# Linear attention block: uneven halves of the state, three head groups folded inside the second half, and another order of the first loads

## The chip, the cores and the metric

The kernel runs on one core of a Trainium2 chip. The metric is the device time in microseconds (us) of one execution. Each execution also leaves a span, from its first to its last recorded instruction, and a granted TensorE clock (1.0 is full speed). The chip has a slower state: a run is called slow when it is over 1.5% above the fastest run of the same kernel.

Engine names in the profile: PE is TensorE (matmuls), PEld its weight loads, DVE is VectorE, ACT is ScalarE, POOL is GpSimd, SP is SyncE, which here only issues DMAs. A *bank* is one of the eight numbered places (0 to 7, 512 columns each) that the kernel writes matmul results to. It is in use until another engine has read the result.

## The reference

```python
B, S, D = 1, 2048, 640;  H = 32;  Dh = 20          # all inputs bf16
q, k, v = split(x @ wqkv)                          # 32 heads of 20
phi = lambda t: where(t > 0, t + 1, exp(t)) + 1e-6
pq, pk = phi(q), phi(k)
kv  = einsum("bhsd,bhse->bhde", pk, v);  z = sum over s of pk
num = pq @ kv;  den = pq . z + 1e-6
out = (num / den) @ wo
```

The kernel uses associativity. It never forms V. It makes the state P = x^T pk (640 x 640), then kv = Wv^T P for each group of heads, masks it to the heads' own 20 x 20 blocks, multiplies it with Wo ("folding Wo", giving w2), and the output is pq (divided by den) times w2.

## The kernel before: the parts that matter

The operations are added in program order to one queue per engine, and semaphores follow from what each reads and writes. **An engine runs its own queue strictly in the order in which the operations were added.** An operation that is not ready holds up everything behind it (seen below: VectorE stood idle for 2.00 us with ready operations queued behind one that was not).

```python
def p_step(h, st, ds=range(5)):          # PE: 5 matmuls for x tile st, P half h (320 columns)
    for d in ds: matmul(bank(d, HALF), xn[tile st, chunk d], pk[st, half h],
                        start=(st == 0), stop=(st == 15))
def p_out(h):                            # P half h -> pt: banks 0,2,4 by ACT, banks 1,3 by DVE
def q_tile(sbk, c, b):                   # PE: 5 matmuls of 512 columns into bank b
    ACT: eq = exp(bank b)
    DVE: eq = min(eq, 1) + 1e-6
    DVE: pq[sbk, c] = max(bank b, 0) + eq          # only now is bank b free
def z_steps():                           # DVE: 7 additions over pk (1280 wide), then zs; ACT zh; DVE zl
def z_finish(b):                         # PE: z per feature; DVE: zc, then five zb = hm * zc
def inverse(pair):                       # PE: den; ACT: ln, exp; SP: spread rd;
                                         #   queues 10 normalisations pq *= rd (DVE)
# ... cut ...
for st in range(2, 16):                  # half one: P holds banks 0-4 open
    p_step(0, st)
    if st % 3 == 2: next z step
    if st in (3, 7, 10, 13): next_q(0)   # Q tiles use banks 5, 6, 7 in turn
p_out(0); next_q(0); next_q(0)
for st in range(16):                     # half two
    p_step(1, st)
    if st in (0, 1, 3): next z step
    if st in (0, 2, 4, 6, 11): next_q(0)
    if st == 7: z_finish(take())
    if st == 9: inverse(0)
    if st == 14: work(4)                 # 4 normalisations
p_out(1); next_q(2); next_q(2)           # Q tile, each followed by 2 normalisations
kv_group(0); kv_mask(0)                  # all six groups of 120 columns
# ... then folding of groups 0 to 5 with the last Q tiles in between, then 16 output tiles
```

## Time and profile before

| | before |
|---|---|
| time, median of 4 runs | 104.77 us (104.47 to 107.26) |
| span of the profiled run, clock | 103.7 us, 1.0 |
| first P matmul to first output matmul | 28.2 to 79.1: 50.9 us |

Lines to recognise in this kernel: L268 is K, L295 is P, L321 to L334 is a Q tile (matmuls, exp, VectorE's two steps), L340 the z additions, L310 the evacuation of P by VectorE, L384 zb, L396 Wv times P, L413 its mask, L420 the folding, L446 den, L478 the output.

The first view is the chain that ended last, in order of time. Its columns are the start, the length, and what ran.

```profile
5.92 2.35 PE ps L268 x16
...
28.38 2.72 PE ps L295 x20
...
34.90 1.08 PE ps L321 x5
...
79.16 2.78 PE ps L478 x20
```

Twenty P matmuls of 320 columns take 2.72 us, so one issues every 0.136 us, and a Q tile of five 512-column matmuls takes 1.08 us (0.216 each). With these spacings everything TensorE has to do between first P and first output matmul adds up to 47.6 us: 21.8 (P) + 21.6 (Q) + 1.6 (Wv times P) + 1.6 (folding) + 0.7 (den) + 0.3 (z). I call this stretch **the middle**. It took 50.9 us. The Trainium skill ("Perfetto Trace Analysis", Identifying the Most-Contended Engine) warns that matmul busy time is no good measure, because pipelined instructions look smaller in the trace than they are. Here the warning holds, but the records look larger: one 320-column record lasts 0.299 us, over twice its spacing.

The second view is TensorE's waits (the warm-up's line at its top left out). Columns: engine and line, what it waited for, us in total, number of waits, longest.

```profile
PE ps L420 <- DVE kvt L413: 0.8, 1, 0.8
PE ps L446 <- DVE zb L384: 0.6, 1, 0.6
PE ps L420 <- DVE w2g L426: 0.5, 1, 0.5
PE ps L295 <- DVE pt L310: 0.4, 1, 0.4
...
PE ps L321 <- issue: 0.2, 1, 0.2
```

Five short waits lie in the middle, 2.5 us together.

### The profile page before, as it was taken

How to read it: one execution, taken by the hardware profiler on the slowest of the kernel's cores; microseconds unless marked ns; L12 is line 12 of the kernel's file. 1: busy time of each engine (PE TensorE's matmuls, PEld its weight loads, DVE VectorE, ACT ScalarE, POOL GpSimd, SP SyncE). 2: the span in 40 equal slices, each digit the busy share in tenths (PEclk: the TensorE clock that was granted, in tenths of full speed). 3: DMA queues.
4: the chain of work that ended last, by engine and by line, in shares of the span. 5: the costliest groups of instructions: out<-in, count | busy, mean ns of one | idle time of the engine just before them, and what ended most of it. 6: DMA issues, size and time to landing. Idle time of an engine off the chain costs nothing.

```text
span 103.7 us, 1779 instructions
## 1 busy us (share of the span) xinstructions
PE 97.6 (94%) x700; PEld 65.0 (63%) x705; DVE 70.6 (68%) x142; ACT 37.8 (36%) x68; POOL 2.5 (2%) x13
## 2 busy tenths in 40 slices
PE   6989999999999999989999799969799999999992
PEld 2467777777776666646666466736355677777771
DVE  0226988888895587799978409797979625866331
ACT  4005555444422112462224131625646253332222
POOL 6300000000000000000000000000000000000000
PEclk9999999999999999999999999999999999999999
DMA  2999998999960000000000013000550135533333
GB/s 67 290 304 189 216 267 255 376 364 363 234 123 0 3 0 0 0 0 3 6 0 0 0 33 68 0 6 0 157 156 3 63 89 141 193 126 126 126 126 126
DMA packets 17076, 11.93 MB, mean 115 GB/s; under 512 B 8621, under 2 KB 17069, under 8 KB 17069
## 3 DMA queue, kind: packets, MB, share of 16 engines
q1 hardware_dynamic: 16349, 11.22, 39.2%
q10 hardware_dynamic: 720, 0.61, 1.9%
q8 instruction: 5, 0.08, 0.3%
q14 instruction: 2, 0.02, 0.1%
HBM read 5.90 MB, written 2.62 MB: 82 GB/s over the span
## 4 chain that ended last, share of the span: by engine, by line
PE 68%; DVE 18%; DMA 4%; ACT 4%; issue 3%; ACTq 0%; DVEq 0%
PE ps L478 21%; PE ps L268 21%; PE ps L295 13%; PE ps L321 10%; DVE pq L334 5%; DVE za L340 4%; DMA wk<-in_wqkv_dram 4%; DVE eq L331 2%; ACT eq L329 2%; DVE pq L471 1%; PE ps L446 1%; DVE zs L361 1%; PE ps L420 1%; ACT pt L307 1%; DVE zl L366 1%
## 5 line engine op out<-in xcount | busy, mean ns | idle before, releaser
L295 PE MATMUL ps<-pk,xn 128*128 128x320 bf16 x160 | 23.9, 299 | 0.4 <-DVE pt L310 0.4
L321 PE MATMUL ps<-xT,wqn 128*128 128x512 bf16 x95 | 23.0, 379 | 0.4 <-issue 0.2
L268 PE MATMUL ps<-wk,xT 128*128 128x320 bf16 x160 | 22.7, 301 | 0.5 <-DMA wk<-in_wqkv_dram 0.3
L478 PE MATMUL ps<-w2p,pq 128*128 128x320 bf16 (+1 forms) x165 | 22.1, 295 | 0.0
L329 ACT ACTIVATE eq<-ps 128x512 bf16<-128x512 f32 x20 | 11.9, 597 | 23.9 <-PE ps L321 23.4
L295 PEld LDWEIGHTS ps<-pk,xn 128*128 128x128 bf16 x160 | 15.4, 98 | 8.2 <-DVE pt L310 0.9
L268 PEld LDWEIGHTS ps<-wk,xT 128*128 128x128 bf16 x160 | 15.4, 98 | 7.2 <-DMA wk<-in_wqkv_dram 1.2
L478 PEld LDWEIGHTS ps<-w2p,pq 128*128 128x128 bf16 x165 | 15.8, 98 | 6.4 <-DVE pq L334 0.4
L281 ACT ACTIVATE ek<-ps 128x640 bf16<-128x640 f32 x16 | 11.3, 704 | 15.8 <-PE ps L268 15.0
L321 PEld LDWEIGHTS ps<-xT,wqn 128*128 128x128 bf16 x100 | 11.6, 118 | 7.8 <-issue 0.3
L503 DVE CAST osb<-ps 128x320 bf16<-128x320 f32 (+1 forms) x16 | 7.7, 481 | 10.1 <-PE ps L478 10.1
L334 DVE SCALAR_TENSOR_TENSOR pq<-ps,eq 128x512 bf16<-128x512 f32 x20 | 13.8, 692 | 0.7
L286 DVE SCALAR_TENSOR_TENSOR pk<-ps,ek 128x640 bf16<-128x640 f32 x16 | 13.2, 825 | 0.6
L331 DVE TENSOR_SCALAR eq<-eq 128x512 bf16<-128x512 bf16 x20 | 5.8, 289 | 9.8 <-ACT eq L329 9.8
L500 ACT CAST osb<-ps 128x320 bf16<-128x320 f32 (+1 forms) x17 | 7.0, 416 | 13.2 <-PE ps L478 11.7
L471 DVE TENSOR_TENSOR pq<-pq,rd 128x512 bf16<-128x512 bf16 x20 | 7.7, 417 | 0.0
L195 DVE COPY xT<-ps 128x256 bf16<-128x256 bf16 (+1 forms) x8 | 2.2, 320 | 6.5 <-PE ps L190 6.5
L283 DVE TENSOR_SCALAR ek<-ek 128x640 bf16<-128x640 bf16 x16 | 5.2, 325 | 2.0 <-ACT ek L281 2.0
L340 DVE TENSOR_TENSOR za<-pk 128x1280 f32<-128x1280 bf16 x4 | 5.9, 1481 | 0.0
L340 DVE TENSOR_TENSOR za<-za 128x1280 f32<-128x1280 f32 x3 | 4.4, 1481 | 0.0
L258 PE MATMUL ps<-const-bfloat16-1.0 128*128 128x512 bf16 (+1 forms) x8 | 3.1, 546 | 0.8 <-PEq L652 0.8
L420 PE MATMUL ps<-wog,kvt 120*120 120x320 bf16 (+1 forms) x12 | 2.4, 308 | 1.3 <-DVE kvt L413 0.8
(37 smaller groups left out, 32.6 us busy)
## 6 DMA issues: line engine op xcount, KB each, us to landing
out_dram<-osb SPq DMA_DIRECT2D x15, 160.0 KB, 1.8
xn<-in_x_dram SPq DMA_DIRECT2D x3, 640.0 KB, 8.0
wqn<-in_wqkv_dram SPq DMA_DIRECT2D x1, 800.0 KB, 5.6
wv<-in_wqkv_dram SPq DMA_DIRECT2D x1, 800.0 KB, 11.2
wog<-in_wo_dram SPq DMA_DIRECT2D x1, 750.0 KB, 13.2
w2p<-w2g SPq DMA_DIRECT2D x5, 150.0 KB
rd<-rdc SPq DMA_DIRECT2D x8, 64.0 KB, 2.2
wk<-in_wqkv_dram SPq DMA_DIRECT2D x3, 160.0 KB, 3.9
```

The source lines that it names most:

```text
L268: r = e.matmul(bank(b + h, HALF), xT[:, c * S + 128 * st:c * S + 128 * st + 128], wk[:, c * D + HALF * h:c * D + HALF * (h + 1)], start=(c ...
L281: P.add("act", lambda e: e.activation(fold(t[:, :]), two_banks(b), ACTF.Exp), reads=banks + ["table"], writes=[("ek", st % 3)])
L286: P.add("dve", lambda e: e.scalar_tensor_tensor(fold(pk[:, st * D:(st + 1) * D]), two_banks(b), 0.0, fold(t[:, :]), ALU.max, ALU.add), rea ...
L295: r = e.matmul(bank(d, HALF), xn[:, st * D + 128 * d:st * D + 128 * d + 128], pk[:, st * D + HALF * h:st * D + HALF * (h + 1)], start=(st ...
L321: r = e.matmul(bank(b), wqn[:, d * D:(d + 1) * D].rearrange("p (q c) -> p c q", c=NC_)[:, c, :], xT[:, d * S + BK * sbk:d * S + BK * (sbk ...
L329: P.add("act", lambda e: e.activation(t[:, :], bank(b), ACTF.Exp), reads=[("bank", b), "table"], writes=[("eq", i)])
L331: P.add("dve", lambda e: e.tensor_scalar(t[:, :], t[:, :], 1.0, 1e-6, ALU.min, ALU.add), reads=[("eq", i)], writes=[("eq", i)])
L334: P.add("dve", lambda e: e.scalar_tensor_tensor(pq[:, c * S + BK * sbk:c * S + BK * (sbk + 1)], bank(b), 0.0, t[:, :], ALU.max, ALU.add), ...
L340: P.add("dve", lambda e: e.tensor_tensor(d_ap, a, b, ALU.add), reads=ra + rb, writes=[dst])
L471: P.add("dve", lambda e: e.tensor_tensor(v, v, rd[i][:, BK * h:BK * (h + 1)], ALU.mult), reads=[("rd", i, 2 * h), ("rd", i, 2 * h + 1), (" ...
L478: r = e.matmul(bank(b, hi - lo), pq[:, c * S + 128 * st:c * S + 128 * st + 128], w2p[:, c * D + lo:c * D + hi], start=(c == 0), stop=(c == ...
L503: P.add("dve", lambda e: e.tensor_copy(osb[j][:, lo:hi], bank(b, hi - lo)), reads=[("bank", b)], writes=keys)
```

## The change

The intent was to hide three of the six head groups' work (Wv times P and folding) inside half two of P. Half one becomes 360 columns, which is exactly three groups of 120, so these groups' state is complete before half two begins. For this the z steps and den moved later, eight Q tiles instead of five went into half two, zb went to GpSimd, and all copies of w2 went to ScalarE. Apart from that, the start loads x tile 0 whole and Wk block 0 beside it.

```diff
+    PW, PO = (3 * GW, D - 3 * GW), (0, 3 * GW)            # 360 and 280 columns
-            for eng, lo in (("sp", 0), ("act", HALF)):    # x tile 0 in two halves
-                ...
-            for eng, what in (("sp", "w01 w23 w34 x24"), ("act", "x12 w12 w45")):
+            for eng, what in (("sp", "x01 w12 w23 w45 x24"), ("act", "w01 x12 w34")):
-                P.add("dve", lambda e, c=c: e.tensor_scalar(
+                P.add("pool", lambda e, c=c: e.tensor_scalar(   # zb
-        order = "k00 t1 k01 k02 k10 k11 k12 k03 k04 k13 t2 k14 t3"
+        order = "k00 k01 t1 k02 k03 k10 k11 k12 k04 k13 t2 k14 t3"
         for st in range(2, NT):
             p_step(0, st)
-            if st % 3 == 2:
+            if st in (3, 6, 9, 12):
                 zst.pop(0)()
-            if st in (3, 7, 10, 13):
+            if st in (4, 7, 10, 13):
                 next_q(0)
         ...
         for st in range(NT):
             p_step(1, st)
-            if st in (0, 1, 3):
+            if st == 2:
+                b = take()
+                kv_group(0, b)                  # groups 0-2
+                kv_mask(0, b)
+            if st in (1, 4, 7, 10):
                 zst.pop(0)()
-            if st in (0, 2, 4, 6, 11):
+            if st % 2:
                 next_q(0)
-            if st == 7:
+            if st in (6, 8, 10):
+                g = st // 2 - 3
+                w2_split(g, take)               # fold group g, two small banks
+                w2_rows(g)
+            if st == 12:
                 z_finish(take())
-            if st == 9:
+            if st == 14:
                 inverse(0)
-            if st == 14:
-                work(4)
         p_out(1)
-        ... (two Q tiles with 2 normalisations each, then all six groups)
+        small[:] = [5, 6, 7]
+        next_q(0)
+        kv_group(1, 4)                          # groups 3-5
+        kv_mask(1, 4)
+        next_q(0)
+        for g in range(3, NG):
+            w2_group(g, 2 * (g - 3))
+            w2_rows(g)
+        small[:] = [6, 7, 0, 1]
         while qs:
-            next_q(1)
+            next_q(2)
```

More of the change, by code (lines that the diff above doesn't have):

```diff
@@ L225, in load_wk @@
             P.add("act", lambda e: e.add_instruction(tl), writes=["table"])
-            for eng, lo in (("sp", 0), ("act", HALF)):
-                P.add(eng, lambda e, lo=lo: e.dma_start(
-                    xn[:, lo:lo + HALF], x[0, 0:128, lo:lo + HALF]),
-                    writes=[("xn", 0, lo)], dma=True)
-            for eng, what in (("sp", "w01 w23 w34 x24"), ("act", "x12 w12 w45")):
+            for eng, what in (("sp", "x01 w12 w23 w45 x24"), ("act", "w01 x12 w34")):
                 for k in what.split():
@@ L241, in xn_keys @@
         def xn_keys(t):
-            return [("xn", t)] if t else [("xn", 0, 0), ("xn", 0, HALF)]
+            return [("xn", t)]
         def load_rest():
@@ L295, in mm @@
                     r = e.matmul(
-                        bank(d, HALF), xn[:, st * D + 128 * d:st * D + 128 * d + 128],
-                        pk[:, st * D + HALF * h:st * D + HALF * (h + 1)],
+                        bank(d, PW[h]), xn[:, st * D + 128 * d:st * D + 128 * d + 128],
+                        pk[:, st * D + PO[h]:st * D + PO[h] + PW[h]],
                         start=(st == 0), stop=(st == NT - 1))
@@ L304, in p_out @@
             for d in range(NC_):
-                dst = pt[:, d * D + HALF * h:d * D + HALF * (h + 1)]
+                dst = pt[:, d * D + PO[h]:d * D + PO[h] + PW[h]]
                 if d % 2 == 0:
-                    P.add("act", lambda e, d=d, dst=dst: e.copy(dst, bank(d, HALF)),
+                    P.add("act", lambda e, d=d, dst=dst: e.copy(dst, bank(d, PW[h])),
                           reads=[("bank", d)], writes=[("pt", d, h)])
                 else:
-                    P.add("dve", lambda e, d=d, dst=dst: e.tensor_copy(dst, bank(d, HALF)),
+                    P.add("dve", lambda e, d=d, dst=dst: e.tensor_copy(dst, bank(d, PW[h])),
                           reads=[("bank", d)], writes=[("pt", d, h)])
@@ L383, in z_finish, with kv_group, mm, kv_mask @@
             for c in range(NC_):
-                P.add("dve", lambda e, c=c: e.tensor_scalar(
+                P.add("pool", lambda e, c=c: e.tensor_scalar(
                     zb[:, 32 * c:32 * c + 32], hm[:, :], zc[:, c:c + 1], None, ALU.mult),
                     reads=["hm", "zc"], writes=[("zb", c)])
-        def kv_group(b):
-            for lo, hi, bb in ((0, 4, b), (4, 6, b + 1)):
-                def mm(e, lo=lo, hi=hi, bb=bb):
-                    for g in range(lo, hi):
-                        n = gsz[g]
-                        m = 128 if g < 5 else n
-                        for d in range(NC_):
-                            r = e.matmul(
-                                bank(bb, n, off=128 * (g - lo), parts=m),
-                                wv[:, d * D + GW * g:d * D + GW * g + m],
-                                pt[:, d * D + GW * g:d * D + GW * g + n],
-                                start=(d == 0), stop=(d == NC_ - 1))
-                    return r
-                P.add("pe", mm, reads=["wv", "wvpad"] + [("pt", d, h) for d in range(NC_)
-                                                         for h in range(2)],
-                      writes=[("bank", bb)])
-        def kv_mask(b):
-            for lo, n, bb, w in ((0, 4, b, GW), (4, 1, b + 1, GW), (5, 1, b + 1, 40)):
-                src = ps[0:w, BK * bb + 128 * (lo % 4):BK * bb + 128 * (lo % 4) + 128 * n] \
+        def kv_group(h, b):
+            def mm(e):
+                for g in range(3 * h, 3 * h + 3):
+                    n = gsz[g]
+                    m = 128 if g < 5 else n
+                    for d in range(NC_):
+                        r = e.matmul(
+                            bank(b, n, off=128 * (g % 3), parts=m),
+                            wv[:, d * D + GW * g:d * D + GW * g + m],
+                            pt[:, d * D + GW * g:d * D + GW * g + n],
+                            start=(d == 0), stop=(d == NC_ - 1))
+                return r
+            P.add("pe", mm, reads=["wv", "wvpad"] + [("pt", d, h) for d in range(NC_)],
+                  writes=[("bank", b)])
+        def kv_mask(h, b):
+            for lo, n, w in ((0, 3, GW),) if h == 0 else ((3, 2, GW), (5, 1, 40)):
+                src = ps[0:w, BK * b + 128 * (lo % 3):BK * b + 128 * (lo % 3 + n)] \
                     .rearrange("p (g j) -> p g j", j=128)[:, :, 0:w]
@@ L413, in kv_mask, with w2_half @@
                 P.add("dve", lambda e, src=src, m=m, dst=dst: e.tensor_tensor(
-                    dst, src, m, ALU.mult), reads=[("bank", bb), "bm"],
+                    dst, src, m, ALU.mult), reads=[("bank", b), "bm"],
                     writes=[("kvt", g) for g in range(lo, lo + n)])
+        def w2_half(g, h, b):
+            n = gsz[g]
+            P.add("pe", lambda e: e.matmul(
+                bank(b, HALF, parts=n), kvt[0:n, GW * g:GW * g + n],
+                wog[0:n, g * D + HALF * h:g * D + HALF * (h + 1)], start=True, stop=True),
+                reads=[("kvt", g), "wog", "wog5"], writes=[("bank", b)])
         def w2_group(g, b):
@@ L419, in w2_group, with w2_split @@
             for h in range(2):
-                P.add("pe", lambda e, h=h: e.matmul(
-                    bank(b + h, HALF, parts=n), kvt[0:n, GW * g:GW * g + n],
-                    wog[0:n, g * D + HALF * h:g * D + HALF * (h + 1)], start=True, stop=True),
-                    reads=[("kvt", g), "wog", "wog5"], writes=[("bank", b + h)])
-            dst = fold(w2g[0:n, g * D:(g + 1) * D])
-            if g % 2:
-                P.add("dve", lambda e: e.tensor_copy(dst, two_banks(b, parts=n)),
-                      reads=[("bank", b), ("bank", b + 1)], writes=[("w2g", g)])
-            else:
-                P.add("act", lambda e: e.copy(dst, two_banks(b, parts=n)),
-                      reads=[("bank", b), ("bank", b + 1)], writes=[("w2g", g)])
+                w2_half(g, h, b + h)
+            P.add("act", lambda e: e.copy(
+                fold(w2g[0:n, g * D:(g + 1) * D]), two_banks(b, parts=n)),
+                reads=[("bank", b), ("bank", b + 1)], writes=[("w2g", g, 0), ("w2g", g, 1)])
+        def w2_split(g, take):
+            n = gsz[g]
+            for h in range(2):
+                b = take()
+                w2_half(g, h, b)
+                lo = g * D + HALF * h
+                P.add("act", lambda e, b=b, lo=lo: e.copy(
+                    w2g[0:n, lo:lo + HALF], bank(b, HALF, parts=n)),
+                    reads=[("bank", b)], writes=[("w2g", g, h)])
         def w2_rows(g):
@@ L437, in w2_rows @@
                 w2g[0:gsz[g], g * D:(g + 1) * D]),
-                reads=[("w2g", g)], writes=[("w2p", g)], dma=True)
+                reads=[("w2g", g, 0), ("w2g", g, 1)], writes=[("w2p", g)], dma=True)
         def den(pair, b):
@@ L586, in bass_standalone__linear_attn_block__prompt_kernel, with pair @@
             p_step(1, st)
-            if st in (0, 1, 3):
+            if st == 2:
+                b = take()
+                kv_group(0, b)
+                kv_mask(0, b)
+            if st in (1, 4, 7, 10):
                 zst.pop(0)()
-            if st in (0, 2, 4, 6, 11):
+            if st % 2:
                 next_q(0)
-            if st == 7:
+            if st in (6, 8, 10):
[3 more added lines that the diff above has]
+            if st == 12:
                 z_finish(take())
-            if st == 9:
+            if st == 14:
                 inverse(0)
-            if st == 14:
-                work(4)
         assert not zst
         p_out(1)
-        next_q(2)
-        next_q(2)
-        kv_group(0)
-        kv_mask(0)
-        small[:] = [5, 6, 7, 4]
-        def fold_wo(g):
-            w2_group(g, 2 * ((g + 1) % 2))
-            w2_rows(g)
-        next_q(0)
-        fold_wo(0)
-        fold_wo(1)
-        next_q(0)
-        fold_wo(2)
-        fold_wo(3)
-        next_q(0)
-        fold_wo(4)
-        fold_wo(5)
-        while qs:
-            next_q(1)
-        out_tile(0, 0)
+        small[:] = [5, 6, 7]
[5 more added lines that the diff above has]
+            w2_group(g, 2 * (g - 3))
+            w2_rows(g)
+        small[:] = [6, 7, 0, 1]
+        while qs:
+            next_q(2)
+        def pair(st):
+            return 2 * ((st + 1) % 4)
+        out_tile(0, pair(0))
+        work(min(2, len(todo)))
+        out_tile(1, pair(1))
         work(len(todo))
-        out_tile(1, 2)
+        small[:] = [1]
         inverse(1)
-        out_tile(2, 0)
-        out_tile(3, 2)
         late = {4: 2, 5: 2, 6: 2, 7: 1, 8: 1, 9: 1, 10: 1}
-        for st in range(4, NT - 1):
-            out_tile(st, 2 * (st % 4) if st > 5 else 2 * (st % 2))
+        for st in range(2, NT - 1):
+            out_tile(st, pair(st))
             work(late.get(st, 0))
         assert not todo
-        out_last(NT - 1, (6, 7, 0))
+        out_last(NT - 1, (0, 1, 2))
         for name, eng in (("sp", nc.sync), ("pool", nc.gpsimd), ("act", nc.scalar),
```

## The prediction

> **What bounds it now.** TensorE's issue stream. In the chain of waits twenty 128x320 matmuls take 2.72 us (0.136 each), five 128x512 1.08 us (0.216 each). The page's 94% busy says little: the Trainium skill ("Perfetto Trace Analysis", Identifying the Most-Contended Engine) warns that matmul busy time is a poor measure, and here the records agree: one 128x320 record lasts 0.299 us though one issues every 0.136. By spacing, the stretch from the first P matmul (28.3) to the first output matmul (79.1) needs 21.8 (P) + 21.6 (Q) + 1.6 (V times P) + 1.6 (folding Wo) + 0.7 (den) + 0.3 (z) = 47.6 us and takes 50.8: only 3.2 us are gaps. The timeline shows them: 0.6 at 46 (P banks leave late behind a 1.4 us z addition), 0.6 at 58 (den waits for zb), about 1.5 between 68 and 75 (folding waits for VectorE). Output (79.1 to 101.8) has none.
>
> **What changes.** Work is the same: 360 + 280 columns are again 640 (estimate 0.153 + 0.119 us a pair). Moved: three head groups (0.8 us kv, 0.8 fold) into half two, eight Q tiles there instead of five, z steps later, zb to GpSimd, all w2 copies to ScalarE.
>
> *Start.* x tile 0 and Wk block 0 land together, Wk block 1 one turn earlier. Before, k01 waited to 5.92 for Wk block 1. The next limit is x tiles 2-3, still fifth on SyncE's queue (landed about 7.5); K of tile 2 starts 1.1 us after their transpose. So 9.19 becomes about 8.6: gain 0.6.
>
> *Gap at 46:* the z addition before p_out is gone: gain 0.6.
>
> *New gaps in half two and after*, from the measured chain "TensorE ends Q, 0.62 to ScalarE's exp done, 0.33, 0.69 pq" (1.64 in all):
> (a) last z step is queued behind the tenth Q: 1.64 + zs 1.3 + zh 0.75 + zl 0.85 is 4.5 us after that Q; TensorE reaches z_finish after 3.3: 1.2 us.
> (b) zc, then five zb on GpSimd before den; the Trainium skill ("GPSIMD Engine Reference", Engine selection) advises VectorE for elementwise; no trace has this operation yet: 0 to 0.8.
> (c) kv for groups 3-5 needs p_out(1), queued behind the Q tile of step 15: 1.64 + two copies 0.8, against one Q (1.08): 1.3.
> (d) the next-to-next Q reuses bank 6 after only 0.8 us of folding: 0.8.
> (e) inverse(0) comes at step 14, so its normalisations follow the last four Q. Each Q + two normalisations take VectorE 1.59 us; the fifth, which output tile 0 needs, ends 5.2 us after the first of these Q; TensorE arrives after 3.2: 1.9.
> Bank-5 reuse: 0.6 in all.
> Gaps 6.2 in place of 3.2.
>
> **Sum.** +3.0 - 0.6 (start) = +2.4 us: 107.3 us, range 105.4 to 108.9. Chances: faster 0.06, same 0.38, slower 0.56. Naively, hiding the fold alone would give 2 us.
>
> **What would show it.** First K of tile 2 near 8.6; P half one about 16.6 us long; no gap before half two; idle TensorE at z_finish <- zl, at den <- zb (GpSimd), at kv <- pt, at a Q <- pq, and before the first output matmul <- normalisation; the first output matmul near 82; output 22.6 us as before. w2p must have landed by then (about 3 us after its issue in this trace).
>
> **What would make it wrong.** VectorE or ScalarE running ahead of my queue order, so (a) or (e) shrink; the x load landing earlier (start gains 1 us or more); 280-column matmuls issuing no faster than 320 (+1.3); GpSimd much slower than 0.3 us each.

## The result, and the profile after

The changed kernel took 110.24 us (median of 4 runs, 109.69 to 111.19) beside 104.77 us for the one before. The ratio is 1.054 (95% interval 1.045 to 1.064). Ratios here are the mean time of one kernel's fast runs over that of the other's fast runs of the same rounds, so not quite the ratio of the medians. It is slower, by more than twice what I had predicted, and outside my range.

| | before | after |
|---|---|---|
| span of the profiled run, clock | 103.7, 1.0 | 108.9, 1.0 |
| K of tile 2 starts | 9.19 | 9.23 |
| the middle (first P to first output matmul) | 50.9 | 55.9 |
| first output matmul to the end | 24.6 | 24.7 |

(The last row is 103.7 - 79.07 and 108.9 - 84.21.) The whole difference is in the middle. In the changed kernel the lines are L265 K, L292 P, L318 to L331 Q, L337 z additions, L307 evacuation of P, L381 zb, L392 Wv times P, L414 folding, L451 den, L476 normalisation, L483 output. These are TensorE's waits:

```profile
PE ps L483 <- DVE pq L476: 2.0, 1, 2.0
PE ps L318 <- DVE pq L331: 1.7, 4, 0.8
PE ps L392 <- DVE pt L307: 1.4, 1, 1.4
PE ps L373 <- DVE zl L363: 1.0, 1, 1.0
PE ps L255 <- PEq L657: 0.8, 1, 0.8
PE ps L451 <- POOL zb L381: 0.7, 1, 0.7
PE ps L191 <- DMA xn<-in_x_dram: 0.5, 1, 0.5
```

Leaving out L255 (the warm-up at the very start) and L191 (the first x load), eight waits with 6.8 us now lie in the middle, in place of five with 2.5 us. The predicted ones are all there, nearly at their predicted sizes. But 6.8 - 2.5 is 4.3, and the middle grew by 5.1 (from 50.85 to 55.95). The chain shows the rest:

```profile
35.60 1.08 PE ps L318 x5
36.68 2.29 PE ps L292 x15
...
49.96 0.79 PE ps L392 x15
...
56.49 1.29 PE ps L318 x5
57.78 0.02 issue
57.81 0.60 ACT eq L326
...
66.83 1.86 POOL zb L381 x5
```

Each L318 piece is the five matmuls of one Q tile. The first is followed by other matmuls, and the chain times it to their start: 1.08 us. The second is followed by ScalarE's exp, which needs the result, and is timed to the end of its last record: 1.29 us. The difference is there because a record outlasts its spacing, by 0.299 - 0.136 = 0.16 us at 320 columns. I call this the drain. Recorded idle time starts only where the last record ends. So one wait costs its recorded idle time and about 0.2 us more. The Trainium skill ("TensorE: Matmul & The Clock Gate", Single matmul latency) gives a drain of about 175 ns, which is of the same size. The ends of matmul records are modelled, so their length is no test of that figure; but the exp did begin only 0.03 us after the modelled end.

That gives a sum that can be tested: **middle = 47.6 + recorded idle + 0.2 x number of waits**. Before: 47.6 + 2.5 + 1.0 = 51.1 (measured 50.9). After: 47.6 + 6.8 + 1.6 = 56.0 (measured 55.9).

The largest wait, in order of time (columns: start, length, engine, line, operation; in brackets the idle time and what ended it):

```profile
78.98 0.60 ACT L326 ACTIVATE eq<-ps 128x512 bf16<-128x512 f32 x1 [0.68 <-PE ps L318]
79.61 0.29 DVE L328 TENSOR_SCALAR eq<-eq 128x512 bf16<-128x512 bf16 x1 [2.00 <-ACT eq L326]
...
83.73 0.75 DVE L476 TENSOR_TENSOR pq<-pq,rd 128x512 bf16<-128x512 bf16 x2
84.21 2.89 PE L483 MATMUL ps<-w2p,pq 128*128 128x320 bf16 x20 [2.03 <-DVE pq L476]
```

VectorE stood idle for 2.00 us at 77.6, although five normalisations could have run then: they stood in its queue behind a Q tile that was not ready. Later TensorE waited for the fifth of them.

The start gained nothing in this pair of traces. The first fence is the chain's start in the kernel before, the second in the changed one:

```profile
1.75 4.12 DMA wk<-in_wqkv_dram
5.87 0.05 issue
5.92 2.35 PE ps L268 x16
8.26 0.29 PE ps L190 x5
```

```profile
1.70 4.47 DMA wk<-in_wqkv_dram
6.18 0.05 issue
6.22 2.08 PE ps L265 x14
8.30 0.29 PE ps L191 x5
```

Two K matmuls fewer were left to do, but the Wk block that the chain waits for landed 0.3 us later. The two cancel. The first K matmul, too, started later: at 4.97 us in place of 4.44, because x tile 0, now one load, was complete at 3.74 in place of 3.13.

### The profile page after: what moved, and what is told of

Read it like the earlier page. It is cut to its first block, busy times and chain, and to the rows that moved or that the text cites. A ratio compares the mean times of both kernels' runs of the same rounds, so it can differ in the third digit from the quotient of the medians.

```text
span 108.9 us, 1781 instructions
## 1 busy us (share of the span) xinstructions
PE 98.0 (90%) x699; PEld 64.4 (59%) x705; DVE 68.0 (62%) x134; ACT 39.6 (36%) x74; POOL 4.4 (4%) x18
## 4 chain that ended last, share of the span: by engine, by line
PE 70%; DVE 13%; ACT 5%; DMA 4%; issue 3%; POOL 2%; SPq 1%
PE ps L483 20%; PE ps L265 20%; PE ps L292 14%; PE ps L318 13%; DVE pq L331 5%; DMA wk<-in_wqkv_dram 4%; ACT eq L326 4%; DVE eq L328 3%; POOL zb L381 2%; DVE pq L476 2%; PE ps L392 2%; DVE za L337 1%; PE ps L451 1%; DVE zs L358 1%; ACT zh L362 1%
## 5 line engine op out<-in xcount | busy, mean ns | idle before, releaser
L318 PE MATMUL ps<-xT,wqn 128*128 128x512 bf16 x94 | 23.2, 381 | 2.0 <-DVE pq L331 1.7
L292 PE MATMUL ps<-pk,xn 128*128 128x360 bf16 (+1 forms) x160 | 24.8, 299 | 0.0
L483 PE MATMUL ps<-w2p,pq 128*128 128x320 bf16 (+1 forms) x165 | 22.1, 295 | 2.0 <-DVE pq L476 2.0
L265 PE MATMUL ps<-wk,xT 128*128 128x320 bf16 x160 | 22.4, 299 | 0.5 <-DMA wk<-in_wqkv_dram 0.3
L483 PEld LDWEIGHTS ps<-w2p,pq 128*128 128x128 bf16 x165 | 15.7, 98 | 8.6 <-DVE pq L476 2.7
L292 PEld LDWEIGHTS ps<-pk,xn 128*128 128x128 bf16 x160 | 15.4, 98 | 8.0 <-issue 0.2
L265 PEld LDWEIGHTS ps<-wk,xT 128*128 128x128 bf16 x160 | 15.4, 98 | 7.1 <-issue 0.6
L318 PEld LDWEIGHTS ps<-xT,wqn 128*128 128x128 bf16 x100 | 11.4, 119 | 10.4 <-DVE pq L331 2.9
L331 DVE SCALAR_TENSOR_TENSOR pq<-ps,eq 128x512 bf16<-128x512 f32 x20 | 13.8, 692 | 0.7
L476 DVE TENSOR_TENSOR pq<-pq,rd 128x512 bf16<-128x512 bf16 x20 | 7.7, 417 | 0.8 <-DMA rd<-rdc 0.8
L337 DVE TENSOR_TENSOR za<-pk 128x1280 f32<-128x1280 bf16 x4 | 5.9, 1480 | 0.0
L337 DVE TENSOR_TENSOR za<-za 128x1280 f32<-128x1280 f32 x3 | 4.4, 1481 | 0.0
L381 POOL TENSOR_SCALAR zb<-hm,zc 128x32 bf16<-128x32 bf16 x5 | 1.9, 393 | 63.2 <-DVE zc L378 63.2
L255 PE MATMUL ps<-const-bfloat16-1.0 128*128 128x512 bf16 (+1 forms) x8 | 3.1, 537 | 0.8 <-PEq L657 0.8
```

The costliest lines, as they stand in the source:

```text
L265: r = e.matmul(bank(b + h, HALF), xT[:, c * S + 128 * st:c * S + 128 * st + 128], wk[:, c * D + HALF * h:c * D + HALF * (h + 1)], start=(c ...
L292: r = e.matmul(bank(d, PW[h]), xn[:, st * D + 128 * d:st * D + 128 * d + 128], pk[:, st * D + PO[h]:st * D + PO[h] + PW[h]], start=(st == ...
L318: r = e.matmul(bank(b), wqn[:, d * D:(d + 1) * D].rearrange("p (q c) -> p c q", c=NC_)[:, c, :], xT[:, d * S + BK * sbk:d * S + BK * (sbk ...
L331: P.add("dve", lambda e: e.scalar_tensor_tensor(pq[:, c * S + BK * sbk:c * S + BK * (sbk + 1)], bank(b), 0.0, t[:, :], ALU.max, ALU.add), ...
L337: P.add("dve", lambda e: e.tensor_tensor(d_ap, a, b, ALU.add), reads=ra + rb, writes=[dst])
L476: P.add("dve", lambda e: e.tensor_tensor(v, v, rd[i][:, BK * h:BK * (h + 1)], ALU.mult), reads=[("rd", i, 2 * h), ("rd", i, 2 * h + 1), (" ...
```

## The experiments

The theory: the work is the same, and the loss is made of waits of TensorE that come from the order on VectorE's and ScalarE's queues and from the three small banks. Rivals: the uneven halves or the start cost something by themselves; GpSimd is the cause; or the moved work itself is the cost.

Run-to-run spread is 1 to 1.5 us even among fast runs, and in some of them the granted clock was 0.984. Part of the spread comes from the start, from late loads and, in one profile, from K matmuls spaced 0.27 us in place of 0.136 up to 9.5 us (pt_first): the time from the first K to the first P matmul was 22.9 to 25.1 us in these profiles. So I compare the middle, read from each trace, and give times beside it.

### Parts of the change on the kernel before: start_only, split_only

```diff
 # start_only = before, with
-  x tile 0 in halves; "w01 w23 w34 x24" / "x12 w12 w45"; order "k00 t1 k01 k02 ..."
+  "x01 w12 w23 w45 x24" / "w01 x12 w34"; order "k00 k01 t1 k02 ..."
 # split_only = before, with
-  bank(d, HALF) ... pk[:, st * D + HALF * h:...]
+  bank(d, PW[h]) ... pk[:, st * D + PO[h]:st * D + PO[h] + PW[h]]    # 360, 280
```

> The kernel before with only the new start (x tile 0 in one load, Wk block 0 beside it, new order of the first K steps). Prediction on record: K of tile 2 starts 0.6 us earlier and the time falls by 0.6 us. Theory from the trace of after: [...]x tile 0 and Wk block 2 land later and TensorE starts K of tile 2 at 9.2 as before, so the time stays within 0.3 us of before. Rival: the start itself costs 1 us or more of the 5.

Measured: 105.55 us beside 105.36, ratio 1.000 (0.990 to 1.011). K of tile 2 started at 9.17. The middle is 51.0 us. The interval is 1.1 us wide on each side, so the times alone do not exclude a gain of 0.6 us. The traces of all runs say more: K of tile 2 starts at 8.99 to 10.20 us (median 9.32, five traces) with the old start, and at 8.67 to 11.09 (median 9.38, eight traces) with the new one. So no gain shows, and no loss. Single traces differ by more than the predicted gain.

> The kernel before with P in halves of 360 and 280 columns and nothing moved. If 280-column matmuls issue in proportion (0.119 us each), the two halves take 12.2 + 9.5 us of TensorE and the time changes only through the waits: half two is shorter, so the z and den waits at step 7 and 9 grow by about 0.8 us together (z chain and zb are the same length). Expected +0.5 to +0.9. Rival: 280 columns issue no faster than 320, then half two takes 1.3 us more and the total is +1.3 or more with no new wait.

Measured: 105.63 us, ratio 1.003 (0.997 to 1.009), middle 51.6 us, 0.7 more than before. The wait of den grew from 0.6 to 1.1 us, and a new one of 0.2 us at z_finish appeared:

```profile
PE ps L447 <- DVE zb L385: 1.1, 1, 1.1
...
PE ps L377 <- DVE zl L367: 0.2, 1, 0.2
```

This is 0.5 + 0.2 of idle, as the theory has it. 280 columns issue in proportion, and the rival falls.

### One cause at a time in the changed kernel: zb_vector, bank_only, pt_first, norm_early

```diff
 # zb_vector
-                P.add("pool", lambda e, c=c: e.tensor_scalar(     # zb
+                P.add("dve", lambda e, c=c: e.tensor_scalar(
 # bank_only
-        small[:] = [6, 7, 0, 1]
+        small[:] = [7, 0, 1, 6]
 # pt_first
-            if st % 2:
+            if st % 2 and st < 15:
                 next_q(0)
 ...
         p_out(1)
+        next_q(0)
 # norm_early
         kv_mask(1, 4)
-        next_q(0)
+        work(3)
+        next_q(2)
```

> The changed kernel with the five zb multiplications back on VectorE. Theory (order of the queues, each wait costing its idle time plus about 0.2 us of pipeline drain): the wait of den on GpSimd (0.7 us of idle) goes, gain 0.8 to 1.0 us out of 5.4. Rival (GpSimd is the main cause, also by holding up VectorE): gain 2 us or more.

Measured: 109.90 us, ratio 1.043 (1.037 to 1.050); middle 55.2 us, 0.7 less. The wait of den is gone, all the others are unchanged. GpSimd took 1.86 us for the five small multiplications (the chain above), VectorE takes 0.78:

```profile
67.58 0.78 DVE L381 TENSOR_SCALAR zb<-hm,zc 128x32 bf16<-128x32 bf16 x5
```

So GpSimd is one of eight waits and not the main cause.

> The changed kernel with only the order of the small banks for the last four Q tiles changed from 6,7,0,1 to 7,0,1,6. The wait of TensorE at the first of them (0.82 us) goes. If waits add up, gain 1.0 us. If the next wait takes part of it: ScalarE still copies three w2 groups before it reaches that Q tile's exp, so the normalisations and the first output matmul come only about 0.5 us earlier and the wait before the first output matmul grows from 2.0 to about 2.5.

Measured: 110.55 us, ratio 1.047 (1.037 to 1.057); middle 55.2 us, 0.8 less. (The median time did not fall: of the four runs one was slow and one fast run had a clock of 0.984. The profiled run, at full clock, took 109.88.) The expectation of a half-absorbed gain was not met in full: the wait at the Q tile went (waits on Q from 1.7 to 0.9 us), and the wait before the first output matmul grew only from 2.0 to 2.1:

```profile
PE ps L483 <- DVE pq L476: 2.1, 1, 2.1
...
PE ps L318 <- DVE pq L331: 0.9, 3, 0.3
```

> The changed kernel with the Q tile of step 15 issued after the evacuation of P half two, so that the copies to pt no longer stand behind its exp and VectorE work. Measured from the first P matmul to the first output matmul (55.9 us in the changed kernel, 50.9 before). If this wait is its own: the 1.4 us of idle at kv of groups 3-5 goes with its 0.2 of drain, 1.4 to 1.6 us gained. If waits only move: a later wait grows by as much and less than 0.5 is gained.

Measured: 109.08 and 109.91 us in its two fast runs (ratio 1.041, 1.036 to 1.047); two more runs were slow, at 112.3 and 112.4, and the profile fell on a slow one. Its middle can still be read, since the granted clock was full there and fell only in the output. In this view the first two numbers are the bounds of the stretch; the third from the end is the clock:

```profile
30.10:84.50 54.40, 49.16 (x334) 30.37 (x331) 36.47 (x64) 20.09 (x39) 1.85 (x5) 1.00 0.08 22
84.50:111.00 26.50, 24.53 (x185) 16.75 (x185) 13.35 (x33) 7.79 (x19) 0.00 (x0) 0.94 0.34 109
```

The middle was 54.4 us, 1.5 less, as expected for 1.4 of idle and its drain. The wait of Wv times P is gone from the view of waits, and the one on bank 6 after it shrank from 0.8 to 0.5 us.

> The changed kernel with the first five normalisations placed before the last four Q tiles on VectorE's queue (three after the mask of groups 3-5, two after the next Q tile), where VectorE is idle in the trace. If the order is the cause: the wait before the first output matmul (2.0 us) goes, 2.0 to 2.2 us gained between first P and first output matmul, and what ends last there is then the landing of the folded Wo. If VectorE's total work is the cause (rival), the wait stays over 1 us.

Measured: 109.22 us, ratio 1.041 (1.036 to 1.045); middle 53.9 us, 2.1 less. The output matmuls now follow the Q tiles without idle time:

```profile
77.49 4.51 PE L318 MATMUL ps<-xT,wqn 128*128 128x512 bf16 x20 [0.82 <-DVE pq L331]
81.94 1.25 PE L483 MATMUL ps<-w2p,pq 128*128 128x320 bf16 x8
```

VectorE's total work is unchanged. Only the order changed. The rest of that expectation, that the landing of w2 would be last there, did not show.

### A fix that only moves the wait: z_early

```diff
-            if st in (3, 6, 9, 12):     # half one, next z step
+            if st % 3 == 2:
-            if st in (1, 4, 7, 10):     # half two, next z step
+            if st in (0, 1, 3):
-            if st == 12:                # z_finish
+            if st == 7:
-            if st == 14:                # inverse(0)
+            if st == 9:
```

> The changed kernel with z additions, z_finish and inverse at the steps of the kernel before (last z step at 3, z_finish 7, den 9). The waits at z_finish (1.0) and den (0.7) go. If waits add up: 2 us gained. Rival: the z additions then stand on VectorE's queue in front of the Q tiles of steps 1 to 5, whose three banks the folded groups also use, so TensorE waits for banks instead, and nothing is gained (within 0.5 us).

Measured: 109.94 and 110.23 us in its two fast runs (two more were slow), ratio 1.047 (1.043 to 1.050); middle 56.3 us, 0.4 more. The two waits went, and so did the three small ones on bank 5. A wait of 0.3 us before half two came back, and a new line stands in the view of waits:

```profile
PE ps L414 <- DVE pq L331: 2.5, 3, 1.5
```

The folding of a group inside half two needs two of the three small banks, and these were held by Q tiles that VectorE had not finished. At the longest of the three waits (1.5 us) it was late because of the z steps. So the rival was right that nothing is gained, and right about the cause of this wait. The two shorter ones (0.8 and 0.2 us) have another cause: no z step ran then. z_finish and den each take a bank of the rotation too, and from their new places they shift it, so that the second half of a group met the bank of the Q tile issued just before (argued from the code and the trace, not tested by itself). In this order, early z steps, eight Q tiles and folding inside half two do not fit together on VectorE and three banks.

### Three together: three_waits

It is bank_only, pt_first and norm_early together.

> The changed kernel with bank order, pt first and early normalisations together. Theory (order of queues): the three waits of 0.8, 1.4 and 2.0 us with 0.2 of drain each go, less about 1 us for the landing of the folded Wo that now comes last before the output: 3.5 to 4 us gained, 52 us between first P and first output matmul, so close to the kernel before and not faster. Rival (the work moved is itself the cost): less than 2 us gained.

Measured: 107.14 us (106.90 to 107.52), ratio 1.019 (1.016 to 1.022); middle 52.4 us, 3.5 less. The last wait before the output is 0.6 us. The view puts it down to VectorE, which had finished 0.25 us earlier, with a Q tile that this output doesn't need. Its fifth normalisation had ended at 78.2 us. The last recorded semaphore update of w2's transfers stands at 80.78 in the trace and the output starts at 80.98, so the landing of w2 was probably last, as expected. The rival (the work itself) falls: three changes of order without any change of work gave back 3.5 of the 5.1 us.

### The same operations in an order without waits: order_outside, order_inside, order_halves

If order is the whole cause, an order without waits must reach 47.6 us. I wrote the middle as a list of tokens, one per operation, and searched for an order by laying the operations out with the durations of the traces. Only the chip's runs are used as evidence. Both kernels keep the halves of 360 and 280 columns, the start of the kernel before, and zb on VectorE.

```diff
-        for st in range(2, NT): ...      # the fixed loops of the middle
+SCHED = (   # order_outside. p: P step; Qb: Q tile in bank b; Z: z step; O: p_out; Khb: Wv times P
+    # and mask, half h; F: z_finish; I: den; Wg..: fold group g; N: one normalisation
+    "Q5 p p Z Q7 p p p p Q7 p Z Q6 Z p p "
+    "p Z p Q6 Z p p p O Q6 Q7 p p Q5 p p "
+    "p p Z Q7 p Z p p Z p p Q7 p p p p "
+    "p O K06 F0 Q7 Q5 W020 K14 W217 I2 Q0 N N W32 N N "
+    "W44 Q1 N W56 Q3 W145 Q2 Q7 Q0 Q5 Q6 "
+)
+        for tok in SCHED.split(): ...     # calls the same functions as before
 # order_inside: the same, with its own list; there K0 and W1 stand inside half two
 # order_halves: order_outside with
-    PW, PO = (3 * GW, D - 3 * GW), (0, 3 * GW)
+    PW, PO = (HALF, HALF), (0, HALF)      # and Wv times P reads both halves
```

> The start of before, zb on VectorE, 360/280 halves, and a new order of the same operations: z additions in steps where VectorE is idle, five Q tiles in half one, two between the halves, three in half two and ten after it, bank by bank; all six head groups fold after half two, between those Q tiles; z_finish and den after half two. Theory (waits made by the order of VectorE's and ScalarE's queues are the whole difference): with no wait of TensorE between first P and first output matmul that stretch takes 47.6 to 48.5 us against 50.9 before and 55.9 in the changed kernel, and the time falls 2.5 to 3 us below before. Rival (folding outside half two costs what the change set out to save): no faster than before.

Measured: 102.52 us (102.14 to 103.28) beside 105.23, correct, ratio 0.977 (0.972 to 0.981), so 1.9 to 2.8% below the kernel before: clearly faster, though at the 2% mark its verdict is "unclear". The middle is 28.0 to 76.2, 48.2 us. Its page says

```profile
PE 97.5 (97%) x699; PEld 65.2 (65%) x705; DVE 68.6 (68%) x139; ACT 39.5 (39%) x74; POOL 2.5 (3%) x13
```

and its view of TensorE's waits has one line, the warm-up:

```profile
PE ps L268 <- PEq L661: 0.8, 1, 0.8
```

VectorE is as busy as before (68%), and no wait of TensorE for it is long enough (0.15 us) for the view. All copies of w2 are on ScalarE here as in the changed kernel, so that move is not the cost either. The expected stretch and the expected gain of 2.5 to 3 us both came out.

> The same as the run beside it, but with the V times P product of groups 0 to 2 and the folding of group 1 inside half two and den at the end of half two. Theory: also no waits, 47.6 to 48.5 us, within 0.5 us of the run beside it, so whether groups fold inside or after half two does not matter once TensorE does not wait. Rival (the intent of the change): inside is faster by about 1 us or more.

Measured: 102.63 us (101.59 to 103.44), correct, ratio 0.974 (0.970 to 0.979): faster than before. The profiled run was a slow one, with 1.4 us of wait for a Wk block at the start. Its middle, which comes after that and ran at full clock, is 48.0 us. So there is no difference to see between folding inside and after half two. What the change set out to hide costs nothing extra outside, once TensorE has no waits there.

> The kernel of order_outside with P in two halves of 320 columns again; the product V times P of groups 0 to 2 then needs both halves. If the split is of no use by itself: within 0.3 us of order_outside (48.2 us between first P and first output matmul). If its use is that groups 0 to 2 need only half one and can run while half two is evacuated: TensorE waits for the copies to pt before that product, about 1.4 us idle plus 0.2, and the stretch becomes 49.5 to 50.3 us, still shorter than before (50.9).

Measured: 105.22 us (104.67 to 105.78) beside 105.24, ratio 1.001 (0.997 to 1.005); middle 50.8 us, a little above the expected range. Two waits that order_outside does not have:

```profile
PE ps L405 <- DVE pt L320: 1.2, 1, 1.2
PE ps L496 <- DVE eq L341: 0.9, 1, 0.9
```

The first (L405 is Wv times P) is the expected one, with 1.2 us of idle. The second (L496 is the output) I had not foreseen. The view puts it down to VectorE, but what this output needs of VectorE was done by 77.9 us, and the output started at 79.14. The transfers of w2 were issued from 73.16 us, in order_outside from 70.45, and the last recorded update of theirs stands at 78.78. So it was probably the landing of w2, made late by the first wait. So the uneven halves do have a use, though not the intended one: groups 0 to 2 need only half one, and their product fills the time in which half two is copied out. In this order, built for the uneven halves, equal ones cost the whole gain. Whether another order would suit equal halves as well stays open.

### The sum, over all runs

"Idle" adds the waits of the middle as the view of waits rounds them, from 0.2 us up.

| run | idle | waits | 47.6 + idle + 0.2 x waits | measured |
|---|---|---|---|---|
| before | 2.5 | 5 | 51.1 | 50.9 |
| start_only | 2.4 | 5 | 51.0 | 51.0 |
| split_only | 3.0 | 6 | 51.8 | 51.6 |
| after | 6.8 | 8 | 56.0 | 55.9 |
| zb_vector | 6.1 | 7 | 55.1 | 55.2 |
| bank_only | 6.2 | 7 | 55.2 | 55.2 |
| pt_first | 5.2 | 7 | 54.2 | 54.4 |
| norm_early | 4.9 | 7 | 53.9 | 53.9 |
| z_early | 7.0 | 7 | 56.0 | 56.3 |
| three_waits | 3.3 | 6 | 52.1 | 52.4 |
| order_halves | 2.3 | 3 | 50.5 | 50.8 |
| order_inside | 0.2 | 1 | 48.0 | 48.0 |
| order_outside | 0 | 0 | 47.6 | 48.2 |

All but the last agree within 0.3 us. In the last, 0.6 us is missing; of this, 0.26 us stands just before the output, whose first matmul starts 0.48 us after the last of the Q tiles in place of 0.22, too little for the view. The rest is not accounted for. The 0.2 was read from the traces after the result, so the table is a description that holds over these runs. No run measured the drain by itself.

## Why the prediction was wrong

The direction and the places were right, the size was not: +2.4 us predicted, +5.5 measured by the medians (+5.2 by the spans).

- **Right: what the middle needs.** 47.6 us; an order without waits took 48.2.
- **Right: "Gap at 46".** The wait for P's banks before half two is gone.
- **Right: 280 columns.** They issue in proportion (half one took 16.5 us against 16.6 predicted; split_only).
- **Right: the five new waits, nearly at size.** Idle, predicted and measured: (a) z_finish 1.2 and 1.0; (b) den 0 to 0.8 and 0.7; (c) Wv times P 1.3 and 1.4; (d) bank 6 0.8 and 0.8; (e) first output matmul 1.9 and 2.0. Reuse of bank 5 was 0.6 and 0.9.
- **Wrong: "Gaps 6.2 in place of 3.2".** The two numbers were counted in different ways. The 3.2 of before came from spacing (50.8 - 47.6), so it included the drain of its waits. The 6.2 was a sum of idle times, without any drain. Counted by spacing, the gaps after are 55.9 - 47.6 = 8.3. Of the missing 2.1 us, 0.6 is idle time that I had put too low (6.8 in place of 6.2, mostly den and bank 5), and the rest is the drain of eight waits, estimated at 0.2 each. This is the term that was mis-sized.
- **Wrong: "So 9.19 becomes about 8.6: gain 0.6".** It became 9.23. I had named x tiles 2 and 3 as the next limit. In the trace TensorE met two others before them. It idled 0.5 us for x tile 0, so that the first K matmul came at 4.97 in place of 4.44 (in all eight traces with the new start at 4.83 to 5.04, in all five with the old one at 4.40 to 4.50). And a Wk block landed 0.3 us later than the one that the kernel before waited for. How late the Wk blocks land differs from run to run: z_early, with the new start, had K of tile 2 at 8.67. The likely reason for the later landing is that the early loads share the DMA engines. The Trainium skill says so ("DMA: Bandwidth & Descriptors", Issuing engines are not separate DMA queues: loads issued from several engines run on the same 16 DMA engines, and issuing from two saves only issue time). The runs show the later landing, not its cause.

With 0.6 for the start and 2.1 for the gaps the prediction would have been 110.0 us.

## What to carry to other kernels

Before moving work into a stretch that looks free, write down the queues of the other engines for that stretch in program order, and ask of each operation on the busiest engine which queue entry stands ahead of what it needs. VectorE at 62 to 68% here held up TensorE eight times with one order, and hardly at all with another, at the same work. Count a gap of TensorE as its recorded idle plus one drain (0.2 us here), and count it the same way on both sides of a comparison. A fix that removes one wait should be tried together with its neighbours: z_early removed five waits (2.6 us of idle), made four others (2.8), and gained nothing.

## What the Trainium skill lacked or had wrong

- "TensorE: Matmul & The Clock Gate", Back-to-back issue gap, gives about 131 ns a matmul of 512 columns and about 81 ns at 128 columns as sustained spacing in real kernels, and says that its formula N/2.4 + 2.5 holds for isolated ones. Here streams of weight loads and matmuls ran at the formula: 216 ns at 512 columns, 136 at 320. Fifteen 120-column matmuls took 0.79 us, 53 ns each.
- The same page gives the drain of a single matmul. No page says that each wait of TensorE therefore costs about 0.2 us more than the idle time that a profile shows (a Q tile takes 1.29 us to its end, 1.08 to the next matmul).
- "GPSIMD Engine Reference", Engine selection, calls operations with one input roughly line-rate on GpSimd. Five 128x32 multiplications by a per-partition scalar took 1.86 us there and 0.78 us on VectorE. With only 32 columns each this may be a fixed cost per instruction and not the rate; no run here tells them apart.
